# Moving batch 2 to paired hidden-layer products in a fused attention and gated-FFN kernel

## The chip, the core and the metric

The kernel runs on one core of a Trainium2 chip. The metric is device time in microseconds: 299.76 us is the median of three runs before the change (299.74 to 299.83). The profile is of one execution of 299.58 us, whose span from first to last instruction is 297.8 us. In the text PE is the matrix engine (TensorE), DVE is VectorE, ACT is ScalarE, POOL is GpSimd, SP issues transfers.

## What is computed

Linear attention over 8 batches of 8 heads, 576 positions and head size 64, then a gated feed-forward layer on the result. `x` has 8 x 576 = 4608 rows of 512; the hidden width is 1536.

```
q_s = softmax over the head size;  k_s = softmax over the positions
x   = q_s @ (k_s^T @ v), per batch and head, heads side by side
g   = x @ w_gate ;  val = x @ w_val
out = (0.5 * g * (1 + erf(g / sqrt 2)) * val) @ w_out
```

## The kernel before

**Blocks.** Of each batch's 576 rows, 512 form one block (0 to 7) and the 64 left over are gathered in `xtr`; eight times 64 make a ninth block of 512, numbered 8. The order is 0, 1, ..., 6, 8, 7. For every block the FFN needs two stages: the hidden layer (gate and value columns, twelve slices of 128 hidden units, results in `ht`) and the output product with `w_out`. The order of the instructions of every engine is the order in which the Python code emits them; nothing is reordered later. The work of the next batch (loads, exponentials, normalisation, the small products that make its `xt`) is hung on named points of the current block by `at(block, kind, point, ...)` and runs where `ride(block, kind, point)` is called. Kinds are FI (after a hidden slice), NS (in the output stage) and PR (a letter in a step list).

**Plain hidden layer.** For each of the twelve slices, four matrix products of 512 columns for the gate and four for the value, L466. ACT applies GELU to the gate (L471), DVE multiplies (L472) into `ht`. Before the change blocks 0, 1 and 2 are made so.

**Paired hidden layer.** Slices k and k+3 are taken together as a 2 x 2 block product with seven products instead of eight (Strassen's method in Winograd's form). Each product is 4 matmuls of 256 columns (`product_gv`, L605). It needs sums of weight halves (`sum_wgv`, L586, in `ws`, and one sum written in place over the weights) and sums of halves of `xt` (`sum_x`, L592, four POOL operations into `xs`). One pair is `pair_step(b, xt, k, i)` with i from 1 to 4. Product 1 goes to bank `pga`, which ACT copies to `pgb` (L660); product 5 goes to `pgc`, whose value is kept as the fifth snapshot `s5` (`snap`, ACT L640 or DVE L638). Then come products 6 (snapshot, ACT), 3, 7, 2 and 4; `add` on DVE (L644) joins them into `cc`, ACT applies GELU (L648, L630) and POOL or DVE multiplies into `ht` (L650, L631). Blocks 3 to 6 follow the list `THREE`: three pairs (k = 0, 1, 2) between the six plain slices 6 to 11. Blocks 8 and 7 follow `SIX`: all six pairs, two of them interleaved, so ACT and DVE have about twice as much of this work for the same PE time.

**Output stage** (`out_strassen`, L712, blocks 1 and later). Seven products again, each 12 matmuls of 256 columns, in banks `psa`, `psb`, `psc`. The order is 1, 2, 5, 6, 3, 7, then what rides on point NS 4, then 4. Product 6 ends in `psa`; its snapshot `s2` is taken before 7 adds into `psa`. `add("c", s2, ...)` joins product 3 and `add("a", s5, ...)` product 7 into the output rows `yo` (both DVE, L750). Product 4 goes on adding into `psa`, so it waits for `add("a")` to have read it. `sum_h` (L575) makes sums of halves of `ht`, part on DVE, part on POOL. `unit_x4`, riding on NS 4, makes the next batch's `xt`: sixteen small products on PE (L429), then ACT copies its quarters 0 and 1 and DVE its quarters 2 and 3 out of PSUM (L190, L192). The next block's first four matmuls need the quarters 0, 1, 2, 3 in that order.

**Weight sums before the change.** The eight sums for k = 0 to 2 are made on DVE during block 2, after its plain slices have used the weights; the eight for k = 6 to 8 are spread over points NS 1 and NS 2 of blocks 3 to 6. `norm_rem0` (a DVE reduction, L270, and a POOL multiplication, L273) rides on NS 4 of block 5 before `sum_x`.

**Buffers.** PSUM banks circulate through the list `ring`; two of eight are kept apart in `att_ring` until `one_ring()` joins them. `cc` has one buffer of its own and a second, `cc_b`, carved out of the exponential buffer of odd batches (`eq_b[1]`), which is free only after batch 3 has been transposed.

Of the kernel before, what the change touches and what calls it, by code (L numbers as in the profile page):

```python
# [18 lines left out]
def kernel(  # L19
# [10 lines left out]
    nc = tc.nc  # L30
# [155 lines left out]
    def copy_on(eng, dst, src):  # L186
        if eng == "pool":
            nc.gpsimd.tensor_copy(out=dst, in_=src)  # L188
        elif eng == "act":
            nc.scalar.copy(out=dst, in_=src)  # L190
        else:
            nc.vector.tensor_copy(out=dst, in_=src)  # L192
# [228 lines left out]
    def unit_x4(b, engs=("act", "dve"), rem=None):  # L421


        xt = get_xt(b)

        def go(ps, hp, src):
            for s in range(2):
                r, t = slice(64 * s, 64 * s + 64), hp % 2
                nc.tensor.matmul(ps[s][64 * t:64 * t + 64], st[(b, "kv4")][r, hp, :], src[r],  # L429
                                 start=True, stop=True)  # L430

        psr = [small([P, 2 + HP, REM], f32, "psxr") for _ in range(2)]
        for hp in range(HP):
            go([p[:, hp // 2] for p in psr], hp, xqr(b, hp))
        if rem is not None:
            for hp in range(HP):
                for s in range(2):
                    r = slice(64 * s, 64 * s + 64)
                    nc.tensor.matmul(psr[s][r, 2 + hp, :], st[(rem, "kv", hp)][r, s, :],
                                     xqr(rem, hp)[r], start=True, stop=True)  # L440
        for s, eng in enumerate(engs):
            copy_on(eng, xtr[:, 2 * s:2 * s + 2, b * REM:(b + 1) * REM], psr[s][:, 0:2])
            if rem is not None:
                r = slice(64 * s, 64 * s + 64)
                copy_on(eng, xtr[r, :, rem * REM:(rem + 1) * REM], psr[s][r, 2:])
        for i in range(2):
            ps = [big([P, MAIN], f32, "psx") for _ in range(2)]
            for hp in (2 * i, 2 * i + 1):
                go(ps, hp, xq(b, hp))
            for s, eng in enumerate(engs):  # L450
                copy_on(eng, xt[:, i + 2 * s, :], ps[s])
# [124 lines left out]

    def sum_wgv(nm, i, k=0, n=NO // 2):
# [6 lines left out]
        nc.vector.tensor_tensor(out=o, in0=a, in1=b, op=op)  # L586

    def sum_x(xt, xs=xs):
        b11, b12, b21, b22 = (xt[:, c:c + 2, r:r + 256] for c in (0, 2) for r in (0, 256))
# [4 lines left out]
    def product_gv(i, ps, xt, k, first):  # L594
# [3 lines left out]
        for t, w, nm in ((0, wv_sb, "v"), (1, wg_sb, "g")):  # L598
# [12 lines left out]
             " 8v 2.3 u1 11g 2.4 11v")  # L611
    SIX = ("0.1 6.1 0.2 6.2 0.3 6.3 0.4 1.1 6.4 7.1 s0 1.2 7.2 1.3 u0 7.3 1.4 2.1 7.4 8.1 s1 2.2"
           " 8.2 2.3 u1 8.3 2.4")
    steps = {b: (SIX if b >= B - 1 else THREE).split() for b in range(3, B + 1)}
    live = {}

    def half(b, xt, c, nm):
# [9 lines left out]
    def pair_step(b, xt, k, i):  # L627
# [24 lines left out]
                op=ALU.mult)  # L652

        if i == 1:
            live["odd"] = odd = not live.get("odd", True)
            cc = cc_b if odd else ffn.tile([P, 2, 2, 256], f32, name="cc", tag="cc", bufs=1)
            pa = big([P, 2, 256], f32, "pga", True)
            product_gv(1, pa, xt, k, True)
            pb = big([P, 2, 256], f32, "pgb", True, True)
            nc.scalar.copy(out=pb, in_=pa)  # L660
            pc = big([P, 2, 256], f32, "pgc", True)
            product_gv(5, pc, xt, k, True)
            live[k] = [cc, pa, pb, pc, snap(pc, k >= NO)]
            return
        cc, pa, pb, pc, s5 = live[k]
        if i == 2:
# [49 lines left out]
    def get_x(b):  # L716
        return get_xt(b) if b < B else xtr

    def last_js(b):
        return (NO - 2 if b < 3 else NO // 2 - 1, NO)  # L720

    def out_strassen(b, last):
        yo = [yop.tile([P, 2, C], f32, name="yo", tag="yo") for _ in range(2)]
# [30 lines left out]
        js = (0, 1, 2, 3, 4, 5) if b < 3 else (0, 3, 1, 4, 2, 5)  # L754
        get("a")
        product(1, ps["a"], True, js=js[:4])
        ride(b, NS, 0)
# [8 lines left out]
        add("b", s1, 0, 0)  # L766
        for x in tiles_["b"]:
            let_go(x)
        sum_h(*last_js(b), (4,), "pool" if b > 2 else "dve")
        get("c")  # L770
        product(5, ps["c"], True, js=js)
        sum_h(*last_js(b), (3,), "pool" if b > 2 else "dve")
        s5 = snap("c")
        ride(b, NS, 1)
        product(6, ps["a"], False, js=js)
        s2 = snap("a")
        ride(b, NS, 2)
        product(3, ps["c"], False, js=js)
        add("c", s2, 0, 1)
        ride(b, NS, 3)  # L780
# [6 lines left out]
        product(7, ps["a"], False, js=js)  # L787
        add("a", s5, 1, 1)
        ride(b, NS, 4)
        if b == B:  # L790
            go_on(B - 1, get_x(B - 1), 1)
# [138 lines left out]
    at(1, FI, 8, L(unit_td, 2))  # L930
    at(1, FI, 11, L(exp, "k", 2, 4, 8), L(exp, "q", 3))
    at(1, NS, 2, L(unit_kv4, 2), L(exp, "k", 3), L(load_batch, 3, ((v, "v"),)), L(cast_v, 3, 0, H))
    at(1, NS, 4, L(unit_x4, 2, ("act", "dve"), 1))
    at(3, FI, 5, L(norm_rem0))
    at(3, FI, 8, L(unit_trem, 0))
    load_2 = lambda n: load_batch(n, ((v, "v"), (q, "q"), (k, "k")))
    at(2, FI, 0, L(load_2, 4))
    for hp in range(HP):
        at(2, FI, hp, L(norm_sum, 3, hp), L(norm_mul, 3, hp, "pool"))
    at(2, FI, 4, L(unit_td, 3))  # L940
    at(2, FI, 5, L(unit_kv4, 3), L(cast_v, 4, 0, H))
    for kind, i, x in ((FI, 4, "g1"), (FI, 5, "g2"), (FI, 6, "v1"), (FI, 9, "g4"), (FI, 10, "v2"),
                       (FI, 11, "g3"), (NS, 1, "v4"), (NS, 2, "v3")):
        at(2, kind, i, L(sum_wgv, x[0], int(x[1])))
    at(2, FI, NFI - 1, L(exp, "q", 4), L(exp, "k", 4))
    for b in range(3, B):
        n = b + 1
        if n < B:
            at(b, PR, "a", L(norm_pair, n, 0, 0, ("pool", "pool")))
            at(b, PR, "n", L(norm_pair, n, 1, 0, ("pool", "pool")))  # L950
            at(b, PR, "t", L(unit_td, n))
        if n + 1 < B:
            at(b, PR, "l", L(load_2, n + 1))
            at(b, NS, 2, L(cast_v, n + 1, 0, H))
            at(b, PR, "e", L(exp, "q", n + 1), L(exp, "k", n + 1))
# [3 lines left out]
    for b in range(2, B - 1):  # L959
        n = b + 1  # L960
        at(b, NS, 4, L(unit_x4, n, ("act", "dve"), 0 if n == B - 1 else None))
        if b == 2:
            at(b, NS, 4, L(unit_kv4, n + 1, True))
        if b == 5:
            at(b, NS, 4, norm_rem0)
        if b > 3:
            at(b, NS, 0, L(unit_kv4, n, True))
        if b == 2:
            at(b, NS, 4, one_ring)
        if b < 6:  # L970
            at(b, NS, 4, L(preload, ACTF.Gelu))
        at(b, NS, 4, L(lambda n: sum_x(get_x(n)), n if n < B - 1 else B))
    at(B, NS, 2, L(lambda: sum_x(get_x(B - 1), xs_b[1])))
    for b in range(3, B + 1):
# [12 lines left out]
    for b in order:  # L987
        xt = get_xt(b) if b < B else xtr
        fi0 = 0
        if b < 2:  # L990
            if b == 0:
                ffn_first0(xt, (x_upper0, L(unit_x, 0, 3, "dve")))
            else:
                ffn_first(xt, first1)
            fi0 = 2 if b == 0 else 3
            ride(b, FI, fi0 - 1)
        if b > 2:
            go_on(b, xt)
        for fi in range(fi0, NFI if b < 3 else 0):
# [49 lines left out]
```

The softmax here doesn't subtract the row's maximum and nothing guards it: scores larger than these inputs give would overflow.

## Time and profile before

| | us |
|---|---|
| device time, median of 3 | 299.76 |
| span of the profile | 297.8 |
| PE busy | 286.4 (96%) |
| DVE / POOL / ACT busy | 218.0 / 181.5 / 179.8 |
| block 2, first hidden matmul to first of block 3 | 81.59 to 113.88 |
| block 4, same | 143.63 to 174.25 |

The page has a busy time per engine, the span in 40 slices, the DMA queues, the chain of work that ended last, and the costliest groups of instructions (line, engine, operation, tiles, count, busy time, mean of one in ns, idle time before). The timeline of an engine lists instructions in order: start, duration, name, and in square brackets the idle time before with what ended it. Matmul ends are modelled and overlap the next start, so the spacing of the starts is what counts: 12 matmuls of 256 columns take 1.31 us from start to start. A wait much shorter than 0.2 us often has no bracket and shows only as a start that comes late.

### The profile page before, as it was taken

Reading aid. Unit: us, or ns where it says so; the run is one execution under the profiler, and the core shown is the slowest. Engines: PE = TensorE matmul, PEld = TensorE weight load, DVE = VectorE, ACT = ScalarE, POOL = GpSimd, SP = SyncE. Lnnn points to the kernel's source line nnn. Section 1 sums busy time; section 2 is a strip of 40 time slices with the busy share of each in tenths; the row PEclk is TensorE's granted clock in tenths of the full one; section 3 lists DMA queues with packets and bytes.
Section 4 is the critical chain, followed back from the end, with each engine's and each line's share of the span. In section 5 each row is a group of like instructions: output and inputs, shape, how many; then the busy total and the mean of one; then the engine's idle time right before and its main releaser. Section 6 shows DMA issues by size and latency. Waiting matters only on the chain. (4 is left out here: it accounts for less than half of the span.)

```text
span 297.8 us, 6098 instructions
## 1 busy us (share of the span) xinstructions
PE 286.4 (96%) x2365; PEld 195.1 (66%) x2365; DVE 218.0 (73%) x410; ACT 179.8 (60%) x287; POOL 181.5 (61%) x166
## 2 busy tenths in 40 slices
PE   3899999999999999999999999998999999999994
PEld 1444445446744586668666866685667888888884
DVE  2953478998768986868686868778577767947792
ACT  3763467776653467667766875685652477438640
POOL 1567557880337008588868776876886366673770
PEclk9999999999999999999999999999999999999999
DMA  7999999997179205960598049802040110033003
GB/s 227 372 383 389 401 390 394 331 317 203 75 261 312 64 2 198 381 128 2 176 380 169 2 142 371 194 2 120 23 93 6 70 75 1 2 72 72 0 2 141
DMA packets 54620, 51.70 MB, mean 174 GB/s; under 512 B 18496, under 2 KB 50496, under 8 KB 54592
## 3 DMA queue, kind: packets, MB, share of 16 engines
q1 hardware_dynamic: 52864, 49.49, 52.2%
q10 hardware_dynamic: 1728, 1.84, 1.9%
q8 instruction: 18, 0.29, 0.4%
q14 instruction: 10, 0.08, 0.1%
HBM read 37.75 MB, written 9.44 MB: 158 GB/s over the span
## 5 line engine op out<-in xcount | busy, mean ns | idle before, releaser
L466 PE MATMUL psg<-xt,wg_sb 128*128 128x512 f16 x240 | 63.6, 379 | 0.0
L466 PE MATMUL psv<-xt,wv_sb 128*128 128x512 f16 x240 | 63.6, 379 | 0.0
L249 POOL TENSOR_TENSOR eq<-eq,rrq 128x640 f16<-128x640 f16 (+1 forms) x27 | 34.8, 1303 | 25.8 <-DVE rrq L242 13.4
L712 PEld LDWEIGHTS <-ht 128*128 128x128 f16 x384 | 37.1, 98 | 8.2 <-issue 2.1
L466 PEld LDWEIGHTS <-wv_sb 128*128 128x128 f16 x240 | 23.4, 98 | 23.8 <-issue 0.2
L471 ACT ACTIVATE gl<-psg 128x512 f32<-128x512 f32 x36 | 21.0, 597 | 29.0 <-PE psg L466 28.9
L466 PEld LDWEIGHTS <-wg_sb 128*128 128x128 f16 x240 | 23.4, 98 | 22.2
L472 DVE SCALAR_TENSOR_TENSOR ht<-psv,gl 128x512 f16<-128x512 f32 x36 | 24.2, 683 | 15.1 <-PE psv L466 12.7
L188 POOL CAST v<-vt 128x640 f16<-128x640 f32 x26 | 21.1, 852 | 12.1 <-PE pskv L342 10.5
L575 POOL TENSOR_TENSOR s<-ht,sh 128x512 f16<-128x512 f16 x18 | 21.8, 1214 | 7.0 <-DVE sh L575 7.0
L650 POOL TENSOR_TENSOR ht<-cc 128x512 f16<-128x512 f32 x12 | 15.4, 1283 | 16.7 <-ACT cc L648 16.5
L575 POOL TENSOR_TENSOR ht<-ht 128x512 f16<-128x512 f16 x18 | 21.5, 1196 | 5.7 <-DVE sh L575 5.7
L605 PEld LDWEIGHTS <-wv_sb 128*128 128x128 f16 x192 | 18.6, 98 | 8.8 <-issue 0.9
L712 PE MATMUL psa<-tw,ht 128*128 128x256 f16 x192 | 23.4, 272 | 0.6 <-DVE yo L750 0.5
L212 ACT ACTIVATE ek<-kt 128x1280 f16<-128x1280 f32 (+1 forms) x11 | 19.1, 1748 | 5.6 <-DMA kt<-in_k_dram 4.1
L592 POOL TENSOR_TENSOR xs<-xt 128x512 f16<-128x512 f16 x8 | 9.2, 1152 | 20.1 <-ACT xt L190 20.1
L630 ACT ACTIVATE glq<-pgb 128x256 f32<-128x256 f32 x24 | 9.1, 380 | 18.9 <-PE pgb L605 12.6
L712 PEld LDWEIGHTS <-sh 128*128 128x128 f16 x192 | 18.8, 98 | 2.4 <-issue 0.2
L605 PEld LDWEIGHTS <-wg_sb 128*128 128x128 f16 x192 | 18.8, 98 | 2.2
L212 ACT ACTIVATE eq<-qt 128x2560 f16<-128x2560 f32 (+2 forms) x10 | 18.4, 1863 | 2.6 <-DMA qt<-in_q_dram 2.5
L660 ACT COPY pgb<-pga 128x512 f32<-128x512 f32 x24 | 14.1, 587 | 9.7 <-PE pga L605 9.5
L631 DVE SCALAR_TENSOR_TENSOR ht<-pga,glq 128x256 f16<-128x256 f32 x24 | 10.1, 420 | 13.2 <-ACT glq L630 13.2
(162 smaller groups left out, 647.4 us busy)
## 6 DMA issues: line engine op xcount, KB each, us to landing
out_dram<-yo SPq DMA_DIRECT2D x15, 512.0 KB, 3.5
kt<-in_k_dram SPq DMA_DIRECT2D x7, 640.0 KB, 8.3
vt<-in_v_dram SPq DMA_DIRECT2D x7, 640.0 KB, 4.9
qt<-in_q_dram SPq DMA_DIRECT2D x7, 640.0 KB, 6.7
qt<-in_q_dram SPq DMA_DIRECT2D x8, 512.0 KB, 7.3
wost<-in_moe_w_out_dram SPq DMA_DIRECT2D x6, 512.0 KB, 7.9
kt<-in_k_dram SPq DMA_DIRECT2D x6, 512.0 KB, 9.6
vt<-in_v_dram SPq DMA_DIRECT2D x6, 512.0 KB, 5.6
```

The source lines that it names most:

```text
L188: nc.gpsimd.tensor_copy(out=dst, in_=src)
L212: nc.scalar.activation(out=dst[:, n0:NC, h0 * D:h1 * D].rearrange(o, d=D, **({"t": 2} if b >= QUAD else {})), in_=heads(tiles[(nm, b)], b, ...
L249: (nc.gpsimd if eng == "pool" else nc.vector).tensor_tensor(out=e, in0=e, in1=rrq.unsqueeze(-1).to_broadcast((P, n, 2, D)), op=ALU.mult)
L466: nc.tensor.matmul(ps, w[:, ci, fi * P:(fi + 1) * P], xt[:, ci, :], start=(ci == 0), stop=(ci == HP - 1))
L471: nc.scalar.activation(out=gl, in_=psg, func=ACTF.Gelu)
L472: nc.vector.scalar_tensor_tensor(out=ht[:, fi, :], in0=psv, scalar=_H_SCALE, in1=gl, op0=ALU.mult, op1=ALU.mult)
L575: (nc.gpsimd if eng == "pool" else nc.vector).tensor_tensor(out=o, in0=a, in1=b, op=op)
L605: nc.tensor.matmul(ps[:, t], a, x, start=(first and t == 0 and c == 0), stop=(c == 1), skip_group_check=True)
L631: nc.vector.scalar_tensor_tensor(out=ht[:, fi, 0:256], in0=ps[:, 0], scalar=_H_SCALE, in1=gl, op0=ALU.mult, op1=ALU.mult)
L650: (nc.vector if k == NFI - NO // 2 - 1 else nc.gpsimd).tensor_tensor(out=ht[:, k:k + NO // 2 + 1:NO // 2, 256:512], in0=cc[:, :, 0], in1=c ...
L660: nc.scalar.copy(out=pb, in_=pa)
L712: nc.tensor.matmul(ps[t], a, w, start=(first and j == js[0] and (t == ts[0] or ps[t].tensor is not ps[ts[0]].tensor)), stop=(j == js[-1]), ...
```

## The change

Block 2 takes the paired hidden layer too. Its weight sums must then exist before it: six go to DVE in block 0 behind the plain slices 5 to 10, and the two that overwrite weights (`g3`, `v3`) go to POOL at the end of block 1's slices. With this the schedule of batches from 2 on becomes the same for all blocks: `sum_x` for batch 2 rides on NS 4 of block 1, `one_ring` comes there too, and the small products for batches 3 and 4 (`unit_kv4`) move to NS 0. Since `cc_b` is not free in block 2, that block uses the single `cc` for its three pairs.

In the output stage of blocks 1 to 5 the last two of the twelve matmuls of product 3 are put behind product 7, so that `add("a")` comes ahead of `add("c")` on DVE, and product 7's twelve matmuls end two matmuls earlier than before. The weight sums for k = 6 to 8 all go to NS 2: two each in blocks 2, 3 and 6, one each in blocks 4 and 5. `norm_rem0` goes behind `sum_x`.

In blocks 8 and 7 all fifth snapshots are taken on DVE, where before those of k = 0 to 2 were on ACT. In block 6 the two copies of batch 0's remainder rows in `unit_x4` are both on ACT.

```diff
-                copy_on(eng, xtr[r, :, rem * REM:(rem + 1) * REM], psr[s][r, 2:])
+                copy_on("act" if b == B - 1 else eng, xtr[r, :, rem * REM:(rem + 1) * REM], psr[s][r, 2:])
...
-    steps = {b: (SIX if b >= B - 1 else THREE).split() for b in range(3, B + 1)}
+    steps = {b: (SIX if b >= B - 1 else THREE).split() for b in range(2, B + 1)}
...
-            live["odd"] = odd = not live.get("odd", True)
+            live["odd"] = odd = b > 2 and not live.get("odd", True)
...
-            live[k] = [cc, pa, pb, pc, snap(pc, k >= NO)]
+            live[k] = [cc, pa, pb, pc, snap(pc, b >= B - 1)]
...
-        product(3, ps["c"], False, js=js)
+        cut = NO - 1 if b < B - 2 else NO
+        product(3, ps["c"], False, js=js[:cut])
+        if cut < NO:
+            product(7, ps["a"], False, js=js)
+            add("a", s5, 1, 1)
+            product(3, ps["c"], False, js=js[cut:])
         add("c", s2, 0, 1)
...
-    at(1, NS, 4, L(unit_x4, 2, ("act", "dve"), 1))
+    at(1, NS, 4, L(unit_x4, 2, ("act", "dve"), 1), one_ring, L(preload, ACTF.Gelu),
+       lambda: sum_x(get_x(2)))
...
-    for kind, i, x in ((FI, 4, "g1"), (FI, 5, "g2"), (FI, 6, "v1"), (FI, 9, "g4"), (FI, 10, "v2"),
-                       (FI, 11, "g3"), (NS, 1, "v4"), (NS, 2, "v3")):
-        at(2, kind, i, L(sum_wgv, x[0], int(x[1])))
-    for b in range(3, B):
+    for i, x in enumerate(("g1", "v1", "g2", "v2", "g4", "v4")):
+        at(0, FI, 5 + i, L(sum_wgv, x[0], int(x[1])))
+    at(1, FI, NFI - 1, L(sum_wgv, "g", 3, 0, NO // 2, "pool"), L(sum_wgv, "v", 3, 0, NO // 2, "pool"))
+    for b in range(2, B):
...
-        if b == 5:
-            at(b, NS, 4, norm_rem0)
-        if b > 3:
-            at(b, NS, 0, L(unit_kv4, n, True))
+        at(b, NS, 0, L(unit_kv4, n, True))
         at(b, NS, 4, L(lambda n: sum_x(get_x(n)), n if n < B - 1 else B))
+        if b == 5:
+            at(b, NS, 4, norm_rem0)
...
-    for b, i, x in ((3, 1, "g1"), (3, 2, "g2"), (4, 1, "v1"), (4, 2, "v2"), (5, 1, "g4"), (5, 2, "v4"),
-                    (6, 1, "g3"), (6, 2, "v3")):
-        at(b, NS, i, L(sum_wgv, x[0], int(x[1]), NO, NO // 2))
+    for b, x in ((2, "g1"), (2, "g2"), (3, "v1"), (3, "v2"), (4, "g4"), (5, "v4"), (6, "g3"), (6, "v3")):
+        at(b, NS, 2, L(sum_wgv, x[0], int(x[1]), NO, NO // 2))
```

More of the change, by code (lines that the diff above doesn't have):

```diff
@@ L575, in sum_h, with sum_wgv @@
             (nc.gpsimd if eng == "pool" else nc.vector).tensor_tensor(out=o, in0=a, in1=b, op=op)
-    def sum_wgv(nm, i, k=0, n=NO // 2):
+    def sum_wgv(nm, i, k=0, n=NO // 2, eng="dve"):
         w = wg_sb if nm == "g" else wv_sb
@@ L585, in sum_wgv @@
                        3: (a21, a11, a21, ALU.subtract), 4: (t[2], a12, t[1], ALU.subtract)}[i]
-        nc.vector.tensor_tensor(out=o, in0=a, in1=b, op=op)
+        (nc.gpsimd if eng == "pool" else nc.vector).tensor_tensor(out=o, in0=a, in1=b, op=op)
     def sum_x(xt, xs=xs):
@@ L719, in last_js @@
     def last_js(b):
-        return (NO - 2 if b < 3 else NO // 2 - 1, NO)
+        return (NO - 2 if b < 2 else NO // 2 - 1, NO)
     def out_strassen(b, last):
@@ L752, in add @@
                     in1=sn[:, t], op0=ALU.mult, op1=ALU.add)
-        js = (0, 1, 2, 3, 4, 5) if b < 3 else (0, 3, 1, 4, 2, 5)
+        js = (0, 1, 2, 3, 4, 5) if b < 2 else (0, 3, 1, 4, 2, 5)
         get("a")
@@ L768, in out_strassen @@
             let_go(x)
-        sum_h(*last_js(b), (4,), "pool" if b > 2 else "dve")
+        sum_h(*last_js(b), (4,), "pool" if b > 1 else "dve")
         get("c")
         product(5, ps["c"], True, js=js)
-        sum_h(*last_js(b), (3,), "pool" if b > 2 else "dve")
+        sum_h(*last_js(b), (3,), "pool" if b > 1 else "dve")
         s5 = snap("c")
@@ L777, in out_strassen @@
         ride(b, NS, 2)
-        product(3, ps["c"], False, js=js)
+        cut = NO - 1 if b < B - 2 else NO
[4 more added lines that the diff above has]
+            product(3, ps["c"], False, js=js[cut:])
         add("c", s2, 0, 1)
-        ride(b, NS, 3)
         for x in tiles_["c"]:
@@ L786, in out_strassen @@
             return
-        product(7, ps["a"], False, js=js)
-        add("a", s5, 1, 1)
+        if cut == NO:
+            product(7, ps["a"], False, js=js)
+            add("a", s5, 1, 1)
         ride(b, NS, 4)
@@ L932 @@
     at(1, NS, 2, L(unit_kv4, 2), L(exp, "k", 3), L(load_batch, 3, ((v, "v"),)), L(cast_v, 3, 0, H))
-    at(1, NS, 4, L(unit_x4, 2, ("act", "dve"), 1))
-    at(3, FI, 5, L(norm_rem0))
-    at(3, FI, 8, L(unit_trem, 0))
+    at(1, NS, 4, L(unit_x4, 2, ("act", "dve"), 1), one_ring, L(preload, ACTF.Gelu),
+       lambda: sum_x(get_x(2)))
     load_2 = lambda n: load_batch(n, ((v, "v"), (q, "q"), (k, "k")))
[L937 to L941, printed above, removed]
-    for kind, i, x in ((FI, 4, "g1"), (FI, 5, "g2"), (FI, 6, "v1"), (FI, 9, "g4"), (FI, 10, "v2"),
-                       (FI, 11, "g3"), (NS, 1, "v4"), (NS, 2, "v3")):
-        at(2, kind, i, L(sum_wgv, x[0], int(x[1])))
-    at(2, FI, NFI - 1, L(exp, "q", 4), L(exp, "k", 4))
-    for b in range(3, B):
+    for i, x in enumerate(("g1", "v1", "g2", "v2", "g4", "v4")):
+        at(0, FI, 5 + i, L(sum_wgv, x[0], int(x[1])))
+    at(1, FI, NFI - 1, L(sum_wgv, "g", 3, 0, NO // 2, "pool"), L(sum_wgv, "v", 3, 0, NO // 2, "pool"))
+    for b in range(2, B):
         n = b + 1
@@ L961 @@
         at(b, NS, 4, L(unit_x4, n, ("act", "dve"), 0 if n == B - 1 else None))
-        if b == 2:
-            at(b, NS, 4, L(unit_kv4, n + 1, True))
-        if b == 5:
-            at(b, NS, 4, norm_rem0)
-        if b > 3:
-            at(b, NS, 0, L(unit_kv4, n, True))
-        if b == 2:
-            at(b, NS, 4, one_ring)
+        at(b, NS, 0, L(unit_kv4, n, True))
         if b < 6:
@@ L972 @@
         at(b, NS, 4, L(lambda n: sum_x(get_x(n)), n if n < B - 1 else B))
+        if b == 5:
+            at(b, NS, 4, norm_rem0)
     at(B, NS, 2, L(lambda: sum_x(get_x(B - 1), xs_b[1])))
-    for b in range(3, B + 1):
+    for b in range(2, B + 1):
         for j in range(NO // 2 - 1):
@@ L996 @@
             ride(b, FI, fi0 - 1)
-        if b > 2:
+        if b > 1:
             go_on(b, xt)
-        for fi in range(fi0, NFI if b < 3 else 0):
+        for fi in range(fi0, NFI if b < 2 else 0):
             ffn_fi(xt, fi, b == 1 and fi == 7)
```

## The prediction

> **What bounds the kernel now.** I read the busy table and the slices first.
>
> ```profile
> PE 286.4 (96%) x2365; PEld 195.1 (66%) x2365; DVE 218.0 (73%) x410; ACT 179.8 (60%) x287; POOL 181.5 (61%) x166
> ...
> PEclk9999999999999999999999999999999999999999
> ```
>
> PE is busy 96% of the span at full granted clock, and the chain that ended last is nearly all PE lines. So time falls only if matmuls disappear or if PE waits less; DVE, ACT and POOL matter only where PE stands behind them. Next, the view of who waited for whom, PE alone:
>
> ```profile
> PE pgc L605 <- POOL xs L592: 0.8, 1, 0.8
> PE psa L712 <- DVE yo L750: 0.5, 3, 0.2
> ...
> PE pga L605 <- ACT pgb L660: 0.3, 2, 0.2
> ```
>
> These are small, but the modelled matmul ends hide part of each. I therefore took the starts of all matmuls in the timeline and compared every step with the usual step of its shape (109.4 ns at 256 columns: 1.3125 us for 12; 216 ns at 512). What starts late by this measure: product 4 in the output stages of blocks 3, 4, 5 by 0.32 each; the first product 5 of block 6 by 0.96; block 8's first product 5 by 0.21; and in the six-pair parts of blocks 8 and 7, matmuls by 0.94 and 0.89 in all. One such place, PE's timeline in block 7:
>
> ```profile
> 280.28 0.38 PE L605 MATMUL pgc<-xt,wsv 128*128 128x256 f16 x2
> 280.49 0.38 PE L605 MATMUL pgc<-xt,wsg 128*128 128x256 f16 x2
> 281.04 0.60 PE L605 MATMUL pga<-vt,kt 128*128 128x256 f16 x4 [0.16 <-ACT pgb L660]
> 281.61 0.60 PE L605 MATMUL pgc<-xt,kt 128*128 128x256 f16 x4
> ```
>
> The third should start at 280.49 + 0.22 = 280.71 and starts at 281.04; the fourth is late by 0.13 more. ACT at that time:
>
> ```profile
> 279.63 0.59 ACT L640 ACTIVATE snq<-pgc 128x512 f32<-128x512 f32 x1
> 280.11 0.38 ACT L630 ACTIVATE glq<-pga 128x256 f32<-128x256 f32 x1
> 280.38 0.61 ACT L660 COPY pgb<-pga 128x512 f32<-128x512 f32 x1
> ```
>
> The copy that PE waits for (280.38) is queued behind the snapshot of pgc (279.63), which is the one that the change gives to DVE.
>
> **What the Trainium skill says.** (1) "TensorE: Matmul & The Clock Gate", Back-to-back issue gap, gives N/2.4 + 2.5 ns: 109 ns and 216 ns for 256 and 512 columns. The trace agrees (1.3125/12 = 0.1094; 0.216). Halving the columns thus costs 2.5 ns per matmul more. (2) "SBUF — State Buffer", Who interferes with whom, says that a VectorE tensor_tensor with both inputs in SBUF contends with GpSimd's reads. The trace agrees: the same sum of 128x768 (L586) takes 0.54 us at best and 1.26 us beside POOL work. (3) "GPSIMD Engine Reference", Elementwise — side-by-side cycle accounting, has 2.6 cycles per element for a two-input sum; between POOL's 1.15 us for 512 elements and 3.36 us for 1536 (L556) the slope is 2.16 ns, which is 2.6 cycles of 1.2 GHz.
>
> **The change part by part.**
>
> 1. *Block 2 in pairs.* Three pairs replace 48 matmuls of 512 columns (10.36 us) by 84 of 256 (9.19), and the last product 4 starts 0.12 late in each such block (132.23, 161.98, 192.60). Check on whole layers: block 2 takes 103.17 - 81.59 = 21.58, less 0.85 for the kv products inside it, 20.73; block 4's pairs take 163.28 - 143.63 = 19.65. Gain **1.08**. The moved kv products cost the same 0.85 at their new places.
>
> 2. *Sums for k = 0 to 2.* Block 0: DVE idles 1.04 between the multiplications of two slices; a sum takes 0.55 to 1.26, so it lags at most 0.22 per slice, 1.3 after six. The six banks hold three slices, and DVE then waits 1.59 for exponentials at 37.6 anyway. POOL's casts of weights finish 2 us before PE reads them. Zero. Block 1: g3 and v3 take 1.15 + 256 x 2.16 ns = 1.70 each on POOL, which is idle from 66.2 to 76.4. Beside them four DVE sums may double, +1.6 at worst; product 6 at 74.56 needs a snapshot now done at 73.1, and product 2's last slice at 73.0 one done at 71.6. Zero, +0.4 at worst.
>
> 3. *Product 7 ahead of the end of product 3.* In blocks 3, 4, 5 product 4 waits for `add("a")` to read psa. Product 7 now ends two matmuls (0.22) earlier; the wait is gone, and product 4 keeps the 0.09 that the turn of tile shape costs anyway (seen at 111.80). Gain 3 x 0.23 = **0.69**. But `add("c")` now follows `add("a")` on DVE, and behind it stand the copies of `xt`. Block 1, DVE:
>
> ```profile
> 79.54 0.69 DVE L750 SCALAR_TENSOR_TENSOR yo<-psa,sn 128x512 f32<-128x512 f32 x1 [0.62 <-PE psa L712]
> 80.15 0.72 DVE L192 CAST xtr<-psxr 128x128 f16<-128x128 f32 x2
> 80.90 1.29 DVE L192 CAST xt<-psx 128x512 f16<-128x512 f32 x2
> ```
>
> The second cast ends at 82.19, and block 2's fourth matmul wants it at 81.59 + 0.65 = 82.24: no slack today. After: add a at 79.32, add c at 79.93, the small casts at 80.54, the large from 81.29, done at 82.57 + 0.05, while PE wants it at 82.15. A new wait of 0.47, less 0.10 won at product 4: **loss 0.37** at the start of block 2. Same reckoning in blocks 2 to 5, with one small cast only: done at 174.73 against 174.71 wanted (block 4). Sums at NS 2 lie between the snapshot of product 6 (done 170.2) and add a (171.98); two of them at 0.55 to 1.1 just fit. I charge 0.05 each, **loss 0.20**.
>
> 4. *norm_rem0 behind sum_x.* In block 5, POOL's first `xs` sum stands behind a multiplication (205.79, 1.04 us) that waited 2.90 for DVE; PE's 0.96 is that. In block 4, without it, `xs` is ready 1.5 before its use. Gain **0.96**. The multiplication runs later, before normalisations on POOL that nobody waits for soon.
>
> 5. *Fifth snapshots.* A snapshot is 0.5 to 0.6 on either engine. ACT's GELU and copy come 0.5 earlier; on DVE the snapshot goes into gaps of 0.86 and 0.70 that today wait for that GELU. Walking the queues: at 245.57 the whole 0.32 goes. At 252.30 DVE's snapshot of pair 2 ends later than ACT's did relative to PE (0.14), the copy too (0.11), and pair 8's by 0.06, so of 0.62 some 0.29 goes. Block 8: 0.61; block 7 likewise 0.26 + 0.30. With 0.10 from the remainder copies at 237.09: **1.27**. DVE's work per two pairs becomes 6 x 0.60 + 6 x 0.33 = 5.6 us against 6.1 of PE, so it stays below.
>
> 6. *Pair 0 to 2 on one `cc`.* In block 3's timing, POOL frees `cc` at 122.6 and the next pair writes at 124.6; then 128.2 and 129.9. Slack 1.7 and more: zero. Bank order, `one_ring` and moved loads: block 2's banks are last read by 82.6 and its third bank is wanted at 84: zero.
>
> Sum: -1.08 - 0.69 - 0.96 - 1.27 + 0.37 + 0.20 = **-3.43**. From 299.76: 296.33; I say **296.3**.
>
> **Rivals.**
>
> *R1, the other engines eat half.* DVE becomes the bound of the six-pair parts (it is unbroken from 252.1 to 261.3 today) and part 5 gives only 0.3; contention in blocks 0 and 1 costs 0.4. -3.43 + 0.97 + 0.4 = -2.06: **297.7**. For it: DVE's chain. Against: the chain starts earlier by as much as PE.
>
> *R2, all late starts go.* Part 5 gives its whole 1.83 + 0.2, and the DVE copies make no wait (parts 3's 0.47 and 0.20 gone): -3.43 - 0.76 - 0.67 = -4.86: **294.9**. Against: block 1's casts have no slack.
>
> *R3, a new wait takes over: slower.* If `cc` in block 2 stands behind POOL (its normalisations, 2.5 us for two, go ahead of a multiplication of 1.3), two pairs wait at least 1.3 each; with block 1's tail late by 0.4 and part 5 turned round (0.25 lost in each six-pair part instead of the gain), -1.08 - 0.69 - 0.96 + 0.57 + 2.6 + 0.4 + 0.5 = +1.34: **301.1**. With waits of 0.6 it comes out about even. Against: the slacks of 1.4 to 2 us in parts 2 and 6.
>
> **Numbers.** My forecast 0.58, R1 0.24, R2 0.09, R3 slower 0.05, about even 0.04. The range 295.4 to 297.8 takes in the forecast, R1 and the unknowns of parts 2, 3 and 5 (+0.4, +-0.4, +-0.7), not R2 and R3. Faster 0.91, same 0.04, slower 0.05.
>
> **What will show it.** PE's waits should no longer list psa behind yo nor pgc behind xs. Block 2's first hidden matmul to block 3's should take some 30.8 and block 4's 30.4. At block 2's start a matmul should stand some 0.4 behind DVE's cast of xt. In blocks 8 and 7 the wait for pgb should shrink, with small waits for DVE's snapshots in its place. POOL should run two sums of 1.7 us near 66 us and PE should not notice. I am wrong if PE stands in block 2 behind `cc` or `ht`, or if blocks 8 and 7 are no shorter.

## The result and the profile after

The changed kernel takes 297.50 us (median of 4 runs, 297.40 to 297.51), the kernel before 299.79 on the same chip (299.74 to 300.01). The ratio is 0.9921, with a 95% interval of 0.9904 to 0.9938: 2.29 us less, where the forecast was 3.46 less.

The busy table of the changed kernel, and its granted clock by slice:

```profile
PE 285.9 (97%) x2401; PEld 198.4 (67%) x2401; DVE 221.0 (75%) x409; ACT 182.0 (62%) x295; POOL 200.5 (68%) x181
...
PEclk9999999999999999999999999999999999999999
```

PE is still the bound, at the same clock. It has 36 matmuls more (84 for 48), but narrower ones, and POOL carries 19 us more. The view of who waited for whom, PE alone (us in total, times, longest), changed more:

```profile
PE psb L712 <- DVE ht L472: 0.3, 1, 0.3
PE psg L466 <- DVE xt L192: 0.2, 1, 0.2
```

The three lines that the prediction quoted from the kernel before (`pgc` behind `xs`, `psa` behind `yo`, `pga` behind `pgb`) are gone. Two waits are new. The second was forecast; the first stood in the prediction only as a worst case. The waits' sizes are understated here because matmul ends are modelled, so I compare the starts of stages in PE's timeline. Block 0 itself began at 14.91 us before and at 15.27 after, with the same instructions ahead of it on every engine (and at 14.94 to 15.34 in the experiments). No edit stands ahead of that point, so stages are compared and not spans. The small products `unit_kv4`, 0.85 us each, are taken out where they moved from block 2 to block 3.

| stage | before | after | difference | forecast |
|---|---|---|---|---|
| block 0 | 33.54 | 33.54 | 0 | 0 |
| block 1, hidden layer | 22.17 | 22.18 | +0.01 | 0 |
| block 1, output stage | 10.97 | 11.30 | +0.33 | -0.10 |
| block 2, hidden layer, less one `unit_kv4` before | 20.73 | 20.17 | -0.56 | -1.08 + 0.47 |
| block 2, output stage | 10.71 | 10.76 | +0.05 | +0.05 |
| blocks 3, 4, 5, less one `unit_kv4` after | 90.99 | 90.43 | -0.56 | -0.69 + 0.15 |
| block 6, hidden layer | 20.60 | 19.68 | -0.92 | -0.96 |
| block 8, both stages | 29.88 | 29.41 | -0.47 | -0.71 |
| block 7, hidden layer | 17.90 | 17.59 | -0.31 | -0.56 |

These differences come to -2.43. Two places carry nearly all of the shortfall: block 1's output stage (+0.43 against forecast) and the six-pair parts of blocks 8 and 7 (0.49 short). The first is visible in PE's timeline of the changed kernel, columns start, duration, engine, line, operation, tiles:

```profile
72.30 1.26 PE L712 MATMUL psb<-wo_sb,ht 128*128 128x256 f16 x10
73.80 0.39 PE L712 MATMUL psb<-wo_sb,ht 128*128 128x256 f16 x2 [0.25 <-DVE ht L472]
```

Ten matmuls at 109.4 ns put the eleventh at 73.39; it starts at 73.80, so 0.41 is lost to an `ht` that DVE makes. The work on DVE and on POOL that came before it:

```profile
67.33 1.26 DVE L575 TENSOR_TENSOR ht<-ht 128x512 f16<-128x512 f16 x1
68.51 1.85 DVE L575 TENSOR_TENSOR s<-ht,sh 128x512 f16<-128x512 f16 x1
...
73.06 0.68 DVE L472 SCALAR_TENSOR_TENSOR ht<-psv,gl 128x512 f16<-128x512 f32 x1
```

```profile
66.49 1.80 POOL L586 TENSOR_TENSOR wg_sb<-wg_sb 128x768 f16<-128x768 f16 x1
68.27 1.81 POOL L586 TENSOR_TENSOR wv_sb<-wv_sb 128x768 f16<-128x768 f16 x1
```

POOL's rows are the moved sums `g3` and `v3`. While they run, two DVE sums of a half-width tile take 1.26 and 1.85 us. They end at 68.58 and 70.36, each 0.28 after the POOL sum beside it (68.30 and 70.08, from unrounded times). DVE's queue is then late up to the last `ht` at 73.06.

The forecast wait at block 2's start, on DVE and then on PE:

```profile
80.11 0.69 DVE L750 SCALAR_TENSOR_TENSOR yo<-psa,sn 128x512 f32<-128x512 f32 x1 [1.66 <-PE psa L712]
80.72 0.68 DVE L750 SCALAR_TENSOR_TENSOR yo<-psc,sn 128x512 f32<-128x512 f32 x1
81.32 0.72 DVE L192 CAST xtr<-psxr 128x128 f16<-128x128 f32 x2
82.07 1.29 DVE L192 CAST xt<-psx 128x512 f16<-128x512 f32 x2
```

```profile
82.29 0.90 PE L466 MATMUL psg<-xt,wg_sb 128*128 128x512 f16 x3
83.41 0.38 PE L466 MATMUL psg<-xt,wg_sb 128*128 128x512 f16 x1 [0.22 <-DVE xt L192]
```

The fourth matmul would start 3 x 0.216 after the first, at 82.94, and starts at 83.41: 0.47 late, as worked out in part 3.

Last, the six-pair part of block 8, DVE of the changed kernel:

```profile
250.98 0.43 DVE L575 TENSOR_TENSOR sh<-ht 128x512 f16<-128x512 f16 x1 [0.21 <-POOL ht L650]
251.32 0.68 DVE L644 SCALAR_TENSOR_TENSOR eq<-pgc,snq 128x512 f32<-128x512 f32 x1
...
252.52 0.68 DVE L644 SCALAR_TENSOR_TENSOR eq<-pga,snq 128x512 f32<-128x512 f32 x1
```

The joins (L644) stand in DVE's queue behind the sum `sh` (the step `s1`), and that sum waits 0.21 for a multiplication on POOL. On PE, product 4 of pair 2 starts at 253.25, 0.25 late, when the join that began at 252.52 is over. Three matmuls before it are late by 0.11, 0.13 and 0.06. So 0.55 us of late starts stay in the last pair, of 0.62 before; those of the middle pair, 0.32, are gone. Together that is 0.39 less.

### The profile page after: what moved, and what is told of

Its sections match the earlier page's. It is cut to its first block, busy times and chain, and to the rows that moved or that the text cites. A ratio compares the mean times of both kernels' runs of the same rounds, so it can differ in the third digit from the quotient of the medians.

```text
span 295.7 us, 6184 instructions
## 1 busy us (share of the span) xinstructions
PE 285.9 (97%) x2401; PEld 198.4 (67%) x2401; DVE 221.0 (75%) x409; ACT 182.0 (62%) x295; POOL 200.5 (68%) x181
## 5 line engine op out<-in xcount | busy, mean ns | idle before, releaser
L466 PE MATMUL psg<-xt,wg_sb 128*128 128x512 f16 x216 | 57.8, 379 | 0.2 <-DVE xt L192 0.2
L466 PE MATMUL psv<-xt,wv_sb 128*128 128x512 f16 x216 | 57.4, 379 | 0.0
L575 POOL TENSOR_TENSOR s<-ht,sh 128x512 f16<-128x512 f16 x21 | 25.3, 1207 | 9.5 <-DVE sh L575 9.5
L575 POOL TENSOR_TENSOR ht<-ht 128x512 f16<-128x512 f16 x21 | 25.2, 1199 | 5.5 <-DVE sh L575 5.5
L650 POOL TENSOR_TENSOR ht<-eq 128x512 f16<-128x512 f32 x12 | 15.4, 1286 | 16.0 <-ACT eq L648 15.8
L471 ACT ACTIVATE gl<-psg 128x512 f32<-128x512 f32 x24 | 13.8, 598 | 16.9 <-PE psg L466 14.7
L630 ACT ACTIVATE glq<-pgb 128x256 f32<-128x256 f32 x27 | 10.3, 380 | 21.9 <-PE pgb L605 14.0
L660 ACT COPY pgb<-pga 128x512 f32<-128x512 f32 x27 | 15.8, 584 | 9.8 <-PE pga L605 9.5
L622 ACT ACTIVATE gl<-psg 128x512 f32<-128x512 f32 x30 | 17.7, 590 | 5.7 <-PE psg L466 5.7
L472 DVE SCALAR_TENSOR_TENSOR ht<-psv,gl 128x512 f16<-128x512 f32 x24 | 16.0, 683 | 6.6 <-PE psv L466 6.5
L240 DVE TENSOR_REDUCE rq<-eq 128x20 f32<-128x1280 f16 (+1 forms) x12 | 17.1, 1428 | 4.7 <-ACT eq L212 4.7
```

Source lines behind the costliest of these rows:

```text
L240: nc.vector.reduce_sum(rq, e, axis=mybir.AxisListType.X)
L466: nc.tensor.matmul(ps, w[:, ci, fi * P:(fi + 1) * P], xt[:, ci, :], start=(ci == 0), stop=(ci == HP - 1))
L472: nc.vector.scalar_tensor_tensor(out=ht[:, fi, :], in0=psv, scalar=_H_SCALE, in1=gl, op0=ALU.mult, op1=ALU.mult)
L575: (nc.gpsimd if eng == "pool" else nc.vector).tensor_tensor(out=o, in0=a, in1=b, op=op)
L622: nc.scalar.activation(out=live[c], in_=t, func=ACTF.Gelu)
L650: (nc.vector if k == NFI - NO // 2 - 1 else nc.gpsimd).tensor_tensor(out=ht[:, k:k + NO // 2 + 1:NO // 2, 256:512], in0=cc[:, :, 0], in1=c ...
```

## The experiments

The theory after the result: (a) POOL's `g3` and `v3` slow DVE's sums in block 1; (b) the changed order in the output stage delays `xt` in block 2; (c) in blocks 8 and 7 what is left is not the fifth snapshot but the order of DVE's queue. The rivals: that the sums are harmless and something else in block 1 is late, that the new order is paid back in every block, and that DVE is simply full in the six-pair parts. e1 to e4 and e10 each change the changed kernel in one place, and e9 puts mends together. e5, e6 and e7 put one part alone into the kernel before; e8 and e11 keep block 2's pairs without the other parts. Where the total matters, the profile's time from block 0's start to the end stands beside the timed median: it is 280.45 us for the changed kernel and 282.89 for the one before.

### e1_sums_late: g3 and v3 moved away from DVE's sums

```diff
+    at(1, NS, 2, L(sum_wgv, "g", 3, 0, NO // 2, "pool"), L(sum_wgv, "v", 3, 0, NO // 2, "pool"))
...
-    at(1, FI, NFI - 1, L(sum_wgv, "g", 3, 0, NO // 2, "pool"), L(sum_wgv, "v", 3, 0, NO // 2, "pool"))
```

> The changed kernel with one edit: the two in-place weight sums g3 and v3 stay on POOL but stand behind the casts of v for batch 3, so they run near 80 to 83.5 us instead of 66.5 to 70. Theory (POOL's sums slow the SBUF sums on DVE, the last multiplication into ht comes late, and product 2 of block 1 stands 0.42 for it): the two DVE sums that took 1.26 and 1.85 return to 0.4 to 0.8, no late matmul inside psb, about 0.4 less than the changed kernel, some 297.1 us. Rival (DVE is late from the sums put into block 0, or block 1 is late by itself): the stall inside psb stays and the time is 297.5. Risk: POOL's xs sums for block 2 start 1.4 later, with 0.2 of slack before the first product 5; then up to 0.3 comes back there.

Measured: 296.95 us (296.82 to 297.06), ratio to the kernel before 0.9904 [0.989, 0.9919], 0.55 less than the changed kernel (0.40 from block 0's start). Block 1's output stage takes 10.88 in place of 11.30. DVE's same two sums, and on POOL the first of the moved sums and the first sum of batch 2's `xs`:

```profile
67.11 0.41 DVE L575 TENSOR_TENSOR ht<-ht 128x512 f16<-128x512 f16 x1
67.44 0.41 DVE L575 TENSOR_TENSOR s<-ht,sh 128x512 f16<-128x512 f16 x1
```

```profile
79.26 1.65 POOL L586 TENSOR_TENSOR wg_sb<-wg_sb 128x768 f16<-128x768 f16 x1
82.45 1.16 POOL L592 TENSOR_TENSOR xs<-xt 128x512 f16<-128x512 f16 x1
```

0.41 for 1.26 and for 1.85, with only POOL's sums taken away from beside them; PE's wait for `ht` is gone. (a) is shown. `xs` is still early enough: block 2's hidden layer takes 20.17, as in the changed kernel.

### e2_no_cut_b1: the old order in block 1's output stage

```diff
-        cut = NO - 1 if b < B - 2 else NO
+        cut = NO - 1 if 1 < b < B - 2 else NO
```

> The changed kernel, but block 1 keeps the old order (product 3 whole, then product 7); blocks 2 to 5 keep the new one. Theory (in block 1 the new order only delays DVE's casts of xt, whose two remainder casts leave no slack): the late fourth matmul of block 2 (0.38 + 0.09) goes, product 4 is late by 0.1 again, net 0.37 less, some 297.1 us. Rival (the casts are late because DVE is behind since the stall in product 2, not because of the order): the wait for xt stays in part, gain under 0.15.

Measured: 297.26 us (297.19 to 297.38), ratio 0.9915 [0.9901, 0.993], 0.24 less than the changed kernel (0.15 from block 0's start). Block 2's hidden layer takes 19.70 for 20.17: the wait for `xt` was 0.47 and was made by the order, so (b) is shown. Not all of it reaches the total: product 4 of block 1 is 0.10 late again, as before the change, and block 2's output stage takes 0.21 more. There DVE shows:

```profile
108.83 1.12 DVE L586 TENSOR_TENSOR kt<-wg_sb 128x768 f16<-128x768 f16 x1
109.99 0.95 DVE L586 TENSOR_TENSOR kt<-kt,wg_sb 128x768 f16<-128x768 f16 x1
110.86 0.68 DVE L750 SCALAR_TENSOR_TENSOR yo<-psa,sn 128x512 f32<-128x512 f32 x1
```

In the changed kernel the first of these sums takes 0.55. Here both are slow, and product 4, which waits for `add("a")`, is later by that 0.21. Each sum ends 0.40 or 0.41 after a POOL cast of `v` that was running (these casts end at 109.55 and 110.53). Two sums at NS 2 just fit, or just don't, by how they fall beside POOL. That was not in my expectation.

### e3_snap_act: fifth snapshots of k = 0 to 2 back on ACT

```diff
-            live[k] = [cc, pa, pb, pc, snap(pc, b >= B - 1)]
+            live[k] = [cc, pa, pb, pc, snap(pc, k >= NO)]
```

> The changed kernel with the fifth snapshots of pairs 0 to 2 in blocks 8 and 7 back on ACT. Theory (the move to DVE is what shortened the six-pair parts, by 0.38 in block 8 beyond the 0.13 of the remainder copies, and by 0.31 in block 7): 0.7 more, some 298.2 us, with waits for pgb as in the kernel before. Rival (block 8 and 7 are shorter for other reasons, such as xs being ready earlier): within 0.2 of 297.5.

Measured: 297.95 us (297.87 to 298.04), ratio 0.9937 [0.992, 0.9954], 0.45 more than the changed kernel (0.68 from block 0's start). The hidden layer of block 8 takes 18.90 for 18.54 and that of block 7 17.89 for 17.59. The snapshots on DVE do gain, but 0.36 and 0.30 where the prediction had 0.61 and 0.56. The 0.14 by which block 8 is still below the kernel before (19.04) belongs to the remainder copies: its first product 5 comes 0.08 late, for 0.21 before.

### e7_snap_only: the same part, alone in the kernel before

```diff
-            live[k] = [cc, pa, pb, pc, snap(pc, k >= NO)]
+            live[k] = [cc, pa, pb, pc, snap(pc, b >= B - 1)]
```

> The kernel before with one edit: all fifth snapshots of blocks 8 and 7 on DVE. Theory: 0.65 to 0.75 less, some 299.05 us, as the undoing in the changed kernel cost 0.45 by the clock and 0.65 by the stages; the middle pair's late matmuls (0.32, 0.26) vanish, the last pair's shrink only from 0.62 to 0.5 because DVE becomes the late one. Rival, the prediction's own sum: 1.17 less, 298.6 us.

Measured: 299.16 us (299.0 to 299.6, ten runs), ratio 0.9979 [0.997, 0.9989]. From block 0's start the whole is 0.64 shorter. Block 8's hidden layer is shorter by 0.38 and block 7's by 0.32, with the same late starts left as in the changed kernel (0.11, 0.13, 0.06 and 0.25 in the last pair of either block). The size of part 5 is thus its own, and not an effect of the other parts.

### e4_u0_late: POOL's sums of step u0 one place later

```diff
-    ... 7.1 s0 1.2 7.2 1.3 u0 7.3 1.4 2.1 7.4 8.1 s1 2.2 ...
+    ... 7.1 s0 1.2 7.2 1.3 7.3 u0 1.4 2.1 7.4 8.1 s1 2.2 ...
```

> The changed kernel with one step of the six-pair list moved: u0 (a sum on DVE and one on POOL) comes after 7.3 instead of before it, so POOL multiplies pair 7 before it makes its sum. Theory (what was left of the gain in the six-pair parts is lost because POOL's sum holds back its multiplication, DVE's sum sh then waits 0.21 for it with all later joins queued behind, and PE's product 4 waits 0.25): DVE's wait for POOL goes, product 4 late by under 0.1 at the end of both parts, 0.3 to 0.5 less, some 297.1 us. Rival (DVE is simply full there): no wait for POOL, but product 4 still late by 0.2 or more, time within 0.1 of 297.5.

Measured: 297.43 us (297.22 to 297.56), ratio 0.992 [0.9905, 0.9935], no difference from the changed kernel. Blocks 8 and 7 take 18.53 and 17.59. POOL's multiplication now comes first, and `s1` no longer waits for it, but DVE's sums run beside POOL:

```profile
247.66 0.98 DVE L575 TENSOR_TENSOR sh<-sh,ht 128x512 f16<-128x512 f16 x1
...
250.42 0.74 DVE L575 TENSOR_TENSOR sh<-ht 128x512 f16<-128x512 f16 x1
```

0.98 and 0.74 in place of 0.41, and each ends 0.28 or 0.29 after the POOL instruction beside it. Product 4 of pair 2 is 0.28 late, for 0.25 in the changed kernel: the wait for POOL was turned into contention with POOL, and PE lost as much. The theory that POOL's place alone decides falls; that the joins start late remains, and the next experiment takes up the queue.

### e10_s1_late: the sum s1 behind the join of pair 2

```diff
-    ... 7.4 8.1 s1 2.2 ...
+    ... 7.4 8.1 2.2 s1 ...
```

> The changed kernel with the step s1 of the six-pair list behind 2.2 instead of before it: DVE joins pair 2's product 3 first and makes the sum sh afterwards, when POOL's multiplication is done. Theory (DVE is an unbroken queue in the last third of both six-pair parts and its order decides; the 0.21 that it stood for POOL and the 0.33 of the sum delayed the joins that PE waits for): the wait of 0.21 goes without POOL work being moved, product 4 is late by under 0.1, 0.3 to 0.5 less, some 297.1 us. Rival (DVE is full, so any order gives the same end of its queue): product 4 or the snapshot after it late by the same 0.25, within 0.1 of 297.5.

Measured: 296.91 us (296.64 to 297.14), ratio 0.990 [0.9885, 0.9915], 0.59 less than the changed kernel (0.54 from block 0's start). Block 8's hidden layer takes 18.29 and block 7's 17.33, 0.25 and 0.26 less. DVE in block 8:

```profile
250.39 0.68 DVE L644 SCALAR_TENSOR_TENSOR eq<-pgc,snq 128x512 f32<-128x512 f32 x1
250.99 0.41 DVE L575 TENSOR_TENSOR sh<-ht 128x512 f16<-128x512 f16 x1
251.32 0.68 DVE L644 SCALAR_TENSOR_TENSOR cc<-pgc,snq 128x512 f32<-128x512 f32 x1
```

The same instructions, no gap: the join goes in the time in which DVE stood for POOL, and product 4 is no longer late. (c) is shown for 0.25 of the late starts; the 0.11, 0.13 and 0.06 ahead of it stay, and no run took them away.

### e5_norm_only: norm_rem0 behind sum_x, alone in the kernel before

```diff
-        if b == 5:
-            at(b, NS, 4, norm_rem0)
         ...
         at(b, NS, 4, L(lambda n: sum_x(get_x(n)), n if n < B - 1 else B))
+        if b == 5:
+            at(b, NS, 4, norm_rem0)
```

> The kernel before with one edit: norm_rem0 rides behind sum_x in block 5. Theory (the 0.96 by which block 6's first product 5 comes late is POOL's multiplication standing in front of the first xs sum, and nothing else depends on its place): 0.9 less than before, some 298.8 us, all of it in block 6's hidden stage. Rival (the multiplication only moves its 1.04 us to a place where a later POOL operation is waited for): under 0.3 less, and PE or ACT waiting for POOL later in block 6.

Measured: 298.89 us (298.63 to 299.05), ratio 0.9965 [0.9951, 0.9979], 0.9 less than before. Block 6's hidden layer goes from 20.60 to 19.65. POOL in the kernel before, and then in this run:

```profile
205.79 1.04 POOL L273 TENSOR_TENSOR eq0r<-eq0r,rrq 64x512 f16<-64x512 f16 x1 [2.90 <-DVE rrq L272]
206.80 1.15 POOL L592 TENSOR_TENSOR xs<-xt 128x512 f16<-128x512 f16 x1
```

```profile
204.80 1.15 POOL L592 TENSOR_TENSOR xs<-xt 128x512 f16<-128x512 f16 x1 [1.47 <-ACT xt L190]
...
209.38 1.03 POOL L273 TENSOR_TENSOR eq0r<-eq0r,rrq 64x512 f16<-64x512 f16 x1
```

With the multiplication behind them, the `xs` sums start as soon as ACT has made `xt`. Part 4 is a gain by itself, of the forecast size.

### e6_cut_only: the new order of products 3 and 7, alone in the kernel before

```diff
-        product(3, ps["c"], False, js=js)
+        cut = NO - 1 if 2 < b < B - 2 else NO
+        product(3, ps["c"], False, js=js[:cut])
+        if cut < NO:
+            product(7, ps["a"], False, js=js)
+            add("a", s5, 1, 1)
+            product(3, ps["c"], False, js=js[cut:])
...
-        product(7, ps["a"], False, js=js)
-        add("a", s5, 1, 1)
+        if cut == NO:
+            product(7, ps["a"], False, js=js)
+            add("a", s5, 1, 1)
```

> The kernel before with one edit: the new order of products in blocks 3, 4 and 5, the weight sums left at NS 1 and NS 2. Theory (the sum at NS 1 stands in front of the snapshot of product 6; with product 7 0.22 earlier that snapshot, done at 170.57 in block 4, is late by 0.1 to 0.15 in blocks 4 and 5): 0.2 gained in block 3, under 0.1 in the other two, 0.3 to 0.4 in all, some 299.4 us. Rival (where the sums stand does not matter): 0.64 less, 299.1.

Measured: 299.76 us (299.62 to 300.08, twelve runs), ratio 1.0001 [0.9992, 1.0009]: nothing. Product 4 does gain its 0.20 to 0.22 in each of blocks 3, 4 and 5, but at the start of block 6 PE, DVE and POOL show:

```profile
208.10 0.38 PE L605 MATMUL pgc<-xs,wsv 128*128 128x256 f16 x2 [1.36 <-POOL xs L592]
```

```profile
203.73 1.28 DVE L192 CAST xt<-psx 128x512 f16<-128x512 f32 x2
204.93 0.67 DVE L270 TENSOR_REDUCE rq<-eq0r 64x8 f32<-64x512 f16 x1
```

```profile
205.91 1.04 POOL L273 TENSOR_TENSOR eq0r<-eq0r,rrq 64x512 f16<-64x512 f16 x1 [3.24 <-DVE rrq L272]
206.91 1.14 POOL L592 TENSOR_TENSOR xs<-xt 128x512 f16<-128x512 f16 x1
```

`add("c")`, now behind `add("a")`, pushes the casts and with them `norm_rem0`'s reduction back; POOL's multiplication waits 3.24 for it (2.90 before), and `xs` behind that. The product that was 0.96 late is now 1.53 late: 0.57 of the 0.64 won is given back. No theory had expected this. In this kernel part 3 is worth its gain only together with part 4, which takes the multiplication out of the way.

### e8_pairs_only: block 2 in pairs, without parts 3, 4 and 5

```diff
-        cut = NO - 1 if b < B - 2 else NO
+        cut = NO
...
-            live[k] = [cc, pa, pb, pc, snap(pc, b >= B - 1)]
+            live[k] = [cc, pa, pb, pc, snap(pc, k >= NO)]
...
-                copy_on("act" if b == B - 1 else eng, xtr[r, :, rem * REM:(rem + 1) * REM], psr[s][r, 2:])
+                copy_on(eng, xtr[r, :, rem * REM:(rem + 1) * REM], psr[s][r, 2:])
```

In the same edit `norm_rem0` stands ahead of `sum_x` again.

> The changed kernel with all but block 2's pairs undone: output stages in the old order everywhere, fifth snapshots of pairs 0 to 2 on ACT, norm_rem0 ahead of sum_x, remainder copies as before. Theory: the hidden layer of block 2 gives 1.03, the stall of product 2 in block 1 from POOL's two sums takes 0.42 back, block 2's product 4 is now late by 0.32 like those of blocks 3 to 5 (0.10 before, where kv products stood between): 0.39 less than before, some 299.35 us. Rival (pairs in block 2 are worth their matmuls, 1.03 to 1.17, and the rest of the change cost something): 298.7.

Measured: 301.23 us (301.02 to 301.33), ratio 1.0043 [1.0028, 1.0058], 1.45 slower than before (1.26 from block 0's start), and far from the expectation. Among PE's waits:

```profile
PE psa L712 <- DVE yo L750: 1.8, 4, 0.8
...
PE psc L712 <- POOL ht L575: 0.3, 1, 0.3
```

In blocks 2 and 3, where two weight sums lie at NS 2, DVE now runs both, then `add("c")`, then `add("a")`, and product 4 is late by 0.91 each time. In the changed kernel the new order hides the second sum. Block 2's own hidden layer is shorter by 1.03 here too. The second wait shown is in block 8's output stage, which takes 0.37 longer than before; the run with the sums spread (e11) does not have it, and why it comes here stays open.

### e11_pairs_spread: the same, with one sum at a point

```diff
-    for b, x in ((2, "g1"), (2, "g2"), (3, "v1"), (3, "v2"), ...
-        at(b, NS, 2, L(sum_wgv, x[0], int(x[1]), NO, NO // 2))
+    for b, i, x in ((2, 1, "g1"), (2, 2, "g2"), (3, 1, "v1"), (3, 2, "v2"), ...
+        at(b, NS, i, L(sum_wgv, x[0], int(x[1]), NO, NO // 2))
```

> As the run with the pairs alone, but with the weight sums for k = 6 to 8 one at a point (NS 1 and NS 2) as in the kernel before. Theory (that run was slow because two sums in a row at NS 2 push add a back by 0.6 each in blocks 2 and 3 when the old order leaves add c in front of it): product 4 of blocks 2 and 3 late by 0.32 and not 0.91, so 1.2 less than that run, some 300.0 us, or 299.5 if the late psc of block 8 goes too. Rival (block 2's pairs themselves make DVE late): still 0.9 late, 301.2.

Measured: 299.70 us (299.44 to 300.26, twelve runs), ratio 0.9997 [0.9989, 1.0006]. Product 4 is late by 0.32 in blocks 2 to 5 as it was in 3 to 5. From block 0's start the whole takes 282.54 against 282.89, 0.35 less, which is 1.03 won in block 2's hidden layer, less 0.43 in block 1 (contention, as in the changed kernel) and 0.26 in block 2's output stage, of which 0.22 is its product 4; the timed medians show 0.1 or nothing. So the part that names the change brings little alone.

### e9_mended: the mends together

The edits of e1, e2 and e10, and in blocks 2 and 3 one of the two sums at NS 2 moved to NS 0, ahead of `unit_kv4`:

```diff
+        if b in (2, 3):
+            at(b, NS, 0, L(sum_wgv, "gv"[b - 2], 1, NO, NO // 2))
         at(b, NS, 0, L(unit_kv4, n, True))
...
-    for b, x in ((2, "g1"), (2, "g2"), (3, "v1"), (3, "v2"), (4, "g4"), (5, "v4"), (6, "g3"), (6, "v3")):
+    for b, x in ((2, "g2"), (3, "v2"), (4, "g4"), (5, "v4"), (6, "g3"), (6, "v3")):
```

> The changed kernel with the edits that paid, put together: g3 and v3 behind the casts of v, block 1 in the old order of products, s1 behind 2.2, and in blocks 2 and 3 the first of the two sums for k = 6 to 8 at NS 0 (in front of the kv products, where DVE stood idle 0.65) so that two never stand together between the snapshot of product 6 and add a. Theory (the four losses are separate): 297.5 - 0.42 - 0.37 - 0.6 = 296.1, no stall in psb, none for xt at block 2, product 4 of block 2 late by 0.1 and not by the 0.33 seen when block 1 alone was put back. Rival (they share a cause, DVE's lateness, and the gains overlap): 296.5 to 296.9.

Measured: 295.98 us (295.93 to 296.33), ratio to the kernel before 0.9875 [0.9861, 0.989]. It is 1.52 us below the changed kernel and 3.8 below the one before. From block 0's start the profiles give 1.20 and 3.64: block 0 began 0.31 earlier here than in the profile of the changed kernel, and its output stage took 0.17 longer. Block 2 takes 19.69 and 10.76, blocks 8 and 7 18.29 and 17.33, as in the single runs, so the four losses were separate. The whole list of PE's waits is:

```profile
PE pswarm L458 <- ACT warm L845: 4.9, 1, 4.9
PE pst L367 <- POOL eq L249: 0.4, 1, 0.4
```

Both are start-up, and stood in the kernel before too. Starts that are late by less than this view shows remain: 0.12, 0.13 and 0.06 in the last pair of blocks 8 and 7, and 0.21 in block 8's output stage. The last one was there before too (0.22, at 260.07) and is missing from the prediction's list; the snapshot on DVE that it waits for stands behind a sum that takes 1.04 us beside POOL.

## Why the prediction was right, and where it was not

The direction, the bound and four of the six parts held. The time lies in the range, but only because the range took in R1: it is 1.2 us above the point and 0.2 from R1. Step by step:

**Part 1 (-1.08).** Right: -1.03, in the changed kernel, in e8 and in e11 alike. Block 2's first hidden matmul to block 3's takes 30.93 (forecast 30.8), block 4's 30.43 (30.4). The missing 0.05 is block 2's last product 4, which starts 0.18 late where the other blocks have the 0.12 that was charged. On the matmul spacing, the Trainium skill, "TensorE: Matmul & The Clock Gate", Back-to-back issue gap, calls the formula that the prediction used the gap of an isolated matmul, and gives about 131 ns for a stream of weight loads and matmuls of 512 columns. Here, with a weight load for every matmul, the streams run at 216 ns, and the measurement decides.

**Part 2 (zero, "+0.4 at worst").** The step that failed is "four DVE sums may double, +1.6 at worst", and from it the choice of zero. The sums did not double; two of them took 3 and 4.5 times as long (0.41 to 1.26 and 1.85), 2.3 us more together. The slack for the last `ht` was 1.4 (73.0 against 71.6); it came 1.8 later against the start of its stage. That cost 0.42, the bad end that I had named and not chosen. The Trainium skill, "SBUF — State Buffer", Who interferes with whom, says of DVE's two-port modes that the other side is fully blocked, and of two-input sums only that they contend with POOL's reads. The traces look like blocking for the sums as well: each of the two ends 0.28 after the POOL sum that ran when it began, while POOL's own sum rose only from 1.65 to 1.80. I had the contention in the prediction, and read its size as a factor (0.54 to 1.26). That 1.26, at 91.43 in the trace before, is a sum that ended 0.41 after a POOL multiplication that had 0.84 left to run. POOL's own cost was misread too, though it changed little: the 3.36 for 1536 elements is half of the 6.72 that two such sums take together, one 3.67 and one 3.08. From the 3.08, the 1.15 for 512 and e1's 1.65 for 768 the slope is some 1.9 ns an element, 2.3 cycles of 1.2 GHz and not the 2.6 that the prediction found confirmed; the measurement decides. Block 0's half of part 2 was right: 33.54 both times.

**Part 3 (-0.69, +0.37, +0.20).** Product 4 gained 0.20 to 0.22 in each of blocks 3, 4 and 5, 0.64 in all. The loss at block 2's start came as worked out: 0.47 for `xt`, less 0.10. The 0.05 charged to each of blocks 2 to 5 came as worked out but smaller: the fourth matmul of blocks 3 to 6, which reads the `xt` quarter that DVE makes last, starts 0.03 or 0.04 late where it was on time before, some 0.12 together. What the part did not see is that it hangs on part 4 (e6: 0.57 given back without it), and that the second sum at NS 2 needs the new order (e8: 0.91 in each of two blocks).

**Part 4 (-0.96).** Right: -0.92 in the changed kernel, -0.95 alone.

**Part 5 (-1.27).** The mechanism was right, the term was mis-sized: 0.82, of which 0.38 and 0.32 are the snapshots (e7) and most of the rest the remainder copies. What failed is "of 0.62 some 0.29 goes": the last pair kept 0.55. The walk through DVE's queue followed snapshots and copies, and left out the sum `s1`, which stands for POOL and holds the joins up behind it. Putting it one place later gave 0.25 and 0.26 (e10). R1's reason, that DVE is the bound there, is not what the runs show: DVE had a gap of 0.21, and with e10's order the same work ends earlier.

**Part 6 (zero).** Right within 0.06: no wait for `cc` stands in any view. Whether the single `cc` has to do with block 2's later product 4 no run tests.

The balance: -3.43, and +0.42 (part 2), +0.45 (part 5), -0.08 (the four charges of 0.05), +0.14 (parts 1, 3 and 4 each some 0.05 smaller), +0.06 in small remainders give -2.44, which is what the profiles show from block 0's start; the timed medians give -2.29. R1 came near partly by luck: one term was right (0.4 of contention), one too dark by 0.5 (part 5 at 0.3, measured 0.82), and that its total still comes within 0.2 is chance. R3 fell: the slacks of parts 2 and 6 that stood against it were there for `cc`, and the tail of block 1 alone is no 2 us.

## What to carry to other kernels

When work is moved to POOL, find every two-input SBUF sum that DVE begins in that time, let it end only some 0.3 us (128x512) or 0.4 us (128x768) after the POOL instruction that is then running, and follow DVE's queue from there to the next instruction that PE waits for; a free POOL is not a free place. A walk through an in-order queue has to include the instructions that look harmless, since one that waits for another engine holds up all behind it. Parts of a change that share a queue are not a sum: try them apart before one is credited or blamed.

## What the runs showed of the hardware that I had not expected

A DVE sum of two 128x512 f16 tiles takes 0.41 us alone and 1.26 or 1.85 beside POOL's 128x768 sum, while POOL's takes 1.65 where no such sum runs (e1) and 1.80 beside them: nearly all of the cost fell on DVE. Other such meetings gave 0.74 and 0.98 (e4), and DVE's 128x768 sums went from 0.55 to 1.12 and 0.95 (e2). No factor fits these, but one rule fits every trace of this case: a two-input sum (L575, L586) that DVE begins while POOL is running ends at its own time, or 0.27 to 0.29 us (128x512) or 0.40 to 0.42 us (128x768) after that POOL instruction ends, whichever is later. All 192 sums of the thirteen traces that took over 0.05 longer than alone do so, beside POOL's casts as well as its sums and multiplications. The trace before had 13 of them, so the cost in block 1 could have been estimated from it. Sums that began with no POOL instruction running took 0.41 to 0.43 and 0.54 to 0.55.

And the first hidden matmul of the program comes anywhere from 14.91 to 15.34 us with the same work ahead of it, as large as several of the effects studied here.
